# Attention with random features and a two-GEMM expert: products summed in PSUM, and projections in 64 rows

## The chip, the cores and the metric

The kernel runs on one core of one Trainium2 chip. A core has a matrix engine (PE; its weight loads are listed as PEld), a vector engine (DVE), an activation engine (ACT), GpSimd (POOL) and a queue processor (SP) that issues the DMAs here. PE writes its sums into PSUM, which the kernel uses as eight banks of 128 x 512 float32 values; DVE and ACT read them out. The metric is the device time of one execution, in microseconds; lower is better.

## The reference

```python
def _attn_ref(q, k, v, omega):            # q, k, v: (8, 8, 576, 64), omega: (128, 64)
    m, D = omega.shape
    scale = 1.0 / np.sqrt(np.sqrt(D))
    q_s, k_s = (q * scale, k * scale)
    def phi(x):
        proj = np.einsum('bhsd,md->bhsm', x, omega)
        sq = np.sum(x * x, axis=-1, keepdims=True) / 2.0
        h = proj - sq
        h = h - np.max(h, axis=-1, keepdims=True)
        return np.exp(h) / np.sqrt(m)
    q_p, k_p = (phi(q_s), phi(k_s))
    kv = np.einsum('bhsm,bhsd->bhmd', k_p, v)
    z = np.sum(k_p, axis=2)
    num = np.einsum('bhsm,bhmd->bhsd', q_p, kv)
    den = np.einsum('bhsm,bhm->bhs', q_p, z)[..., None] + 1e-06
    return (num / den).astype(np.float32)

def _moe_ref(x, w_in, w_out):             # x: (4608, 512) from the attention, w_in: (512, 2048)
    h = x @ w_in                          # GEMM 1
    sp = np.maximum(h, 0.0) + np.log1p(np.exp(-np.abs(h)))
    g = h * erf(sp)
    return (g @ w_out).astype(np.float32) # GEMM 2
```

## The kernel before

**Attention.** Two heads make a pair: 32 pairs, four per batch, 2 x 576 tokens each, which are nine chunks of 128 tokens. The fifth chunk (MID) holds the end of one head and the start of the other. For q and for k the tile `u` has 64 rows of data and 64 rows of their squares (`square`, mostly on POOL), so that one product of 128 rows with `wq` or `wk` (`project`, three chunks per PSUM bank `pp`) gives the projection less the squares. `maximum` (DVE) takes the largest feature of each token, `exponential` (ACT) writes `f`. Then `key_values` sums `kvp`, `turn` transposes `fq` into `pt`, and `attend` makes `nd` (numerators and denominators) in two halves of 288 columns per head. From pair 8 on (WHOLE) operands are split into a high and a low part, and a product is three matmuls: high by high, high by low, low by high. ACT takes log and exponential of the denominators (`rc`), DVE multiplies.

**The expert.** Every batch goes through GEMM 1 and GEMM 2 in two phases; in the trace their PSUM tiles begin with `h` and `o`. In a phase GEMM 1 has four granules (`f` 0 to 3), each of two 128-row blocks by 576 columns. In batches 0 to 2 (`plain1`, PLAIN) a granule is four sums of two products. From batch 3 on (`gemm1`) it is seven products of sums of blocks (PRODUCTS), each of six matmuls of 288 columns, each in a PSUM bank of its own (`hA...`, `hS...`). Banks of GEMM 1 are limited to three at once (CAPS `moe1`). The products are put together in SBUF: one is copied to `hs`, the others are added by DVE, some to two places, with `u2` in between. `chain` applies softplus, erf, the gate (`gs`, `hs`), and splits into `gh` and `gl` for GEMM 2.

**Weights.** A weight arrives as 64-bit words, which `make` turns into float32: `w_bias` (POOL or ACT), a shift and two bit operations (DVE), then `parts` splits high and low (`w_high`, `w_rest`; ACT or POOL, DVE or POOL). This is done once for each of 32 units, from the start to some 243 us, and each made unit is stored in device memory (`wdw`). Later uses fetch it: a unit is 512 KB, a block half of that. A granule of `gemm1` fetches three units and a block.

**The order.** All operations are handed to a planner (`Plan.order`), with costs (COST, LAG), due times, the engines that may run each, and limits on tiles at once (SLOTS, CAPS). It simulates the engines and writes out one fixed order for each of them; an engine runs its list in that order and waits on semaphores. BLOCKS sets how granules of GEMM 1 and output tiles of GEMM 2 (`e`, of the phase before) follow each other; attention of later batches is placed between by due time.

```python
PRODUCTS = (("A11", "B11", (((0, 0), None),)),
            ("S2", "T2", (("U2", (0, 0)),)),
            ("S3", "T3", (((1, 0), "U2"),)),
BLOCKS = (("f", 0), ("f", 1), ("e", 0), ("f", 2), ("e", 1), ("f", 3), ("e", 2), ("e", 3))
```

Every instruction goes through one helper, so nearly all rows of the profile name line 742; tiles tell them apart.

Of the kernel before, what the change touches and what calls it, by code (L numbers as in the profile page):

```python
# [25 lines left out]
D1 = D + 1  # L26
DM, DF = 512, 2048
# [22 lines left out]
PRODUCTS = (("A11", "B11", (((0, 0), None),)),  # L50
            ("S2", "T2", (("U2", (0, 0)),)),
            ("S3", "T3", (((1, 0), "U2"),)),
            ("A12", "B21", (((0, 0), (0, 0)),)),
            ("S1", "T1", (((1, 1), (1, 0)), ((0, 1), "U2"))),
            ("A22", "T4", (((1, 0), (1, 0)),)),
            ("S4", "B22", (((0, 1), (0, 1)),)))


COST = dict(mm=0.132, proj=0.222, tr=0.109, kv=0.222, table=1.3)
LAG = {"T": 0.35, "A": 0.25, "V": 0.25, "G": 0.3, "S": 0.3}  # L60
SLOTS = dict(w=8, u=3, f=2, mx=3, v=2, qh=1, ql=1, kh=1, kl=1, rc=2, xs=4, xh=2, xl=2, u2=2,
             hs=4, gs=2, gh=6, gl=6, os=4, ps=8)
CAPS = dict(st=2, wt=2, cv=2, att=4, moe1=3, moe2=2)
# [26 lines left out]
class Plan:  # L90
# [43 lines left out]
    def order(self, slots, caps):  # L134
# [187 lines left out]
def build(emit):  # L322
# [36 lines left out]
    def parts(t, src, keys):  # L359

        ks = range(2)
        pl.op("whigh", [("A", 0.63, -1e9), ("G", 0.7, WHG)], lambda e: E.w_high(e, t, src),
              reads=keys, writes=[(t, ("h", k)) for k in ks])
        pl.op("wrest", [("V", 0.68, -1e9), ("G", 1.3, 3.0)], lambda e: E.w_rest(e, t, src),
              reads=keys + [(t, ("h", k)) for k in ks], writes=[(t, ("l", k)) for k in ks])

    def make(u, t):
# [8 lines left out]
        pl.op("wshift", [("V", 0.42, -1e9)], lambda e: E.w_shift(w), reads=[(w, 0)], writes=[(w, 0)])  # L376
        pl.op("wsign", [("V", 0.69, -1e9)], lambda e: E.w_sign(st, w), reads=[(st, 0), (w, 0)],
              writes=[(w, 0)])
        pl.op("wtail", [("V", 0.69, -1e9)], lambda e: E.w_tail(st, w), reads=[(st, 0), (w, 0)],
              writes=[(w, 0)])  # L380
        parts(t, lambda: w.ap.bitcast(F32).rearrange("p (k c) -> p k c", k=2), [(w, 0)])
        store(u, t)

    def unit(u, block=None):

        count[0] += 1
        t = pl.tile("w", "w%s_%d" % ("_".join(str(c) for c in u), count[0]),
                    [P, 2 if block is None else 1, 2, BW], F32R,
                    cap=SLOTS["w"] - CAPS["cv"] if clock[0] < starts[2 * PLAIN + 1] else None)
        if u not in stored:  # L390
            make(u, t)
        else:
            d = stored[u]
            fetch(u, t, lambda: d.ap if block is None else d.ap[:, block:block + 1])
# [25 lines left out]
    def weights1(b, ph, fp):  # L420
        if b < PLAIN:
            t0, t1 = (unit(("1", ph, 2 * fp + i)) for i in range(2))
            if b == PLAIN - 1:
                make_sums(ph, fp, t0, t1)
            return {"A11": (t0, 0), "A12": (t0, 1), "A21": (t1, 0), "A22": (t1, 1)}
        t0, s0, s1 = unit(("1", ph, 2 * fp)), unit(("S", ph, fp, 0)), unit(("S", ph, fp, 1))
        t1 = unit(("1", ph, 2 * fp + 1), 1)
        return {"A11": (t0, 0), "A12": (t0, 1), "A22": (t1, 0), "S2": (s0, 0), "S3": (s0, 1),
                "S1": (s1, 0), "S4": (s1, 1)}
# [8 lines left out]
    def early(n):  # L438
        return 5 if n < NP else None

    def load(n, qk):
        a = pairs[n]

        u = a["u" + qk] = pl.tile("hs", f"u{qk}{a['nm']}", [P, S2], F32, "u0") if 0 < n < NP else \
            pl.tile("u", f"u{qk}{a['nm']}", [P, S2])
        parts = 3 if n == 0 else 1
        for i in range(parts):
# [3 lines left out]
        if qk == "k":  # L451
            v = a["v"] = pl.tile("v", "v" + a["nm"], [P, (NC + 1) * D1])
            pl.op("loadv", [("S", 0.1, 1e9)], lambda e: E.v_load(v, a), writes=[(v, 0)],
                  size=P * (NC + 1) * D1 * 4)
        for i in range(parts):
# [7 lines left out]
    def project(n, qk, t0):  # L463
# [5 lines left out]
        for i in range(3):  # L469
            pp = pl.tile("ps", f"pp{qk}{a['nm']}_{i}", [P, 512], F32, "att", early(n))  # L470
            pl.op("proj" + qk, [("T", 3 * COST["proj"], -1e9)], lambda e, i=i, pp=pp: E.project(pp, u, qk, i),
                  reads=[(u, ("x", i)), (u, ("s", i))], writes=[(pp, 0)],
                  plan=pair_time(n, t0 + 0.05 * i))
            pl.op("max" + qk, [("V", 0.56, -1e9)], lambda e, i=i, pp=pp: E.maximum(mx, pp, i),
                  reads=[(pp, 0)], writes=[(mx, i)])
            pl.op("exp" + qk, [("A", 1.1, -1e9)], lambda e, i=i, pp=pp: E.exponential(f, mx, pp, i),
                  reads=[(pp, 0), (mx, i)], writes=[(f, i)], set="exp")

    def key_values(n, t0):
# [16 lines left out]
    def turn(n, t0):  # L496
# [15 lines left out]
    def attend(n, t0):  # L512
        a = pairs[n]
        x = xs[n] = pl.tile("xs", f"xs{a['nm']}", [P, 2, T])
        for j in range(2):
            for t in range(2):
                nd = pl.tile("ps", f"nd{a['nm']}_{j}_{t}", [P, 512], F32, "att", early(n))
                rc = pl.tile("rc", f"rc{a['nm']}_{j}_{t}", [P, T])
                c = range((j * S + t * T) // 384, (j * S + (t + 1) * T - 1) // 384 + 1)
                pl.op("nd", [("T", 0.5 if n < WHOLE else 3 * COST["mm"], -1e9)],  # L520
                      lambda e, j=j, t=t, nd=nd: E.attend(nd, a["kh"], a["kl"], a["qh"], a["ql"], j, t),
                      reads=[(a["kh"], 0), (a["kl"], 0)] + [(a["qh"], i) for i in c]
                      + [(a["ql"], i) for i in c], writes=[(nd, 0)],
                      plan=pair_time(n, t0 + 0.1 * j + 0.05 * t))
                pl.op("ndlog", [("A", 0.5, -1e9)], lambda e, j=j, nd=nd, rc=rc: E.log_den(rc, nd, j),
                      reads=[(nd, 0)], writes=[(rc, 0)], set="exp")
                pl.op("ndexp", [("A", 0.44, -1e9)], lambda e, j=j, rc=rc: E.exp_den(rc, j),
                      reads=[(rc, 0)], writes=[(rc, 0)], set="exp")
                pl.op("divide", [("V", 0.47, -1e9)], lambda e, j=j, t=t, nd=nd, rc=rc: E.divide(x, nd, rc, j, t),
                      reads=[(nd, 0), (rc, 0)], writes=[(x, (j, t))])  # L530
# [53 lines left out]
    def product(hp, where, wn, b, names, xn, more, end):  # L584

        unit_, k = where[wn]
# [9 lines left out]
    def plain1(b, ph, fp):  # L596
        where = weights1(b, ph, fp)
# [438 lines left out]
```

## Time and profile before

| | |
|---|---|
| median of 3 runs | 1103.88 us (1101.33 to 1104.65) |
| the profiled execution | span 1101.4 us from first to last instruction; its device time is not listed apart |
| PE busy | 1074.1 us, 98% |
| DVE, ACT, POOL busy | 715.1, 709.0, 435.1 us |
| granted PE clock | 0.988 in the mean, 0.93 in the first 140 us |
| data moved by DMA | 231.27 MB, mean 210 GB/s |

The profiled span is 2.5 us below the median of the runs. A row of the timeline has the start, the time to the modelled end, engine, line, operation, out<-in, shape and count; what stands in brackets is the idle time before it and what ended it. A plain float32 matmul shows as two records, one of the split operands (high or low) as one.

### The profile page before, as it was taken

What the parts mean: (1) busy time and instruction counts of PE and PEld (TensorE: products, weight loads), DVE (VectorE), ACT (ScalarE), POOL (GpSimd) and SP (SyncE); (2) the same over time, 40 slices, a digit from 0 to 9 for tenths busy, and PEclk for the clock granted to TensorE, in tenths of its full rate; (3) what the DMA queues carried; (4) which work ended last, traced back from release to release, by engine and by line L of the source; (5) the groups of instructions that cost most, each with busy time, mean ns of one, the idle gap of its engine ahead of it and who ended that gap; (6) DMA issues with size and microseconds to landing.
All of it is one profiled execution on the core that took longest, in us unless ns stands there. A gap on an engine that the chain in (4) does not pass through costs nothing.

```text
span 1101.4 us, 21514 instructions
## 1 busy us (share of the span) xinstructions
PE 1074.1 (98%) x8272; PEld 1063.9 (97%) x8272; DVE 715.1 (65%) x1257; ACT 709.0 (64%) x1354; POOL 435.1 (40%) x353
## 2 busy tenths in 40 slices
PE   7798899999999999999999999999999999999998
PEld 6698899999999999999999999999999999999998
DVE  5967789876377575955757566675656766464541
ACT  7777769776578766756647667476566764654440
POOL 6535336210075294822436343343334413252300
PEclk9899899999999999999999999999999999999999
DMA  8546568675557666666666777657765666567771
GB/s 241 174 132 205 173 231 279 198 257 162 171 176 251 205 204 242 190 215 226 216 211 207 225 216 222 211 181 247 232 225 185 214 216 208 193 226 278 254 241 58
DMA packets 70117, 231.27 MB, mean 210 GB/s; under 512 B 8288, under 2 KB 8672, under 8 KB 70016
## 3 DMA queue, kind: packets, MB, share of 16 engines
q1 hardware_dynamic: 69952, 229.84, 63.9%
q8 instruction: 66, 1.08, 0.4%
q14 instruction: 35, 0.29, 0.1%
q0 software_dynamic: 64, 0.07, 0.0%
HBM read 195.26 MB, written 34.60 MB: 209 GB/s over the span
## 4 chain that ended last, share of the span: by engine, by line
PE 91%; DVE 4%; ACT 1%; issue 1%; DMA 1%; SPq 1%; POOL 0%; DVEq 0%
PE o L742 36%; PE h L742 13%; PE hS L742 11%; PE hA L742 8%; PE ppq L742 5%; PE kvp L742 5%; PE ppk L742 5%; PE nd L742 5%; PE pt L742 2%; DVE wt L742 1%; DMA uk<-kT 1%; SPq L742 1%; DVE qh L742 0%; DVE hs L742 0%; DVE mxk L742 0%
## 5 line engine op out<-in xcount | busy, mean ns | idle before, releaser
L742 PE MATMUL o<-gh,w 128*128 128x288 f32 x2048 | 444.8, 298 | 7.8 <-POOL w L742 7.4
L742 PEld LDWEIGHTS o<-gh,w 128*128 128x128 f32 x2048 | 338.9, 188 | 9.0 <-POOL w L742 8.0
L742 PE MATMUL o<-gl,w 128*128 128x288 f32 x1024 | 301.9, 295 | 0.0
L742 PEld LDWEIGHTS o<-gl,w 128*128 128x128 f32 x1024 | 192.7, 188 | 0.2
L742 PE MATMUL h<-xh,w 128*128 128x288 f32 x768 | 178.8, 305 | 0.9 <-ACT hs L742 0.9
L742 PE MATMUL hS<-xh,wS 128*128 128x288 f32 x640 | 165.7, 302 | 1.1 <-issue 1.1
L742 ACT ACTIVATE fk<-ppk,mxk 128x128 f32<-128x128 f32 x288 | 83.3, 371 | 78.0 <-DVE mxk L742 77.6
L742 PEld LDWEIGHTS h<-xh,w 128*128 128x128 f32 x768 | 131.2, 191 | 1.6 <-ACT hs L742 1.3
L742 PE MATMUL hA<-xh,w 128*128 128x288 f32 x480 | 122.1, 299 | 0.0
L742 ACT ACT_TABLE_LOAD x92 | 118.0, 1283 | 2.4 <-PEq L1027 0.7
L742 PEld LDWEIGHTS hS<-xh,wS 128*128 128x128 f32 x640 | 114.8, 189 | 1.3 <-issue 1.3
L742 PE MATMUL h<-xl,w 128*128 128x288 f32 x384 | 113.9, 297 | 0.0
L742 ACT ACTIVATE fq<-ppq,mxq 128x128 f32<-128x128 f32 x288 | 83.2, 371 | 40.0 <-DVE mxq L742 39.5
L742 POOL TENSOR_TENSOR gl<-hs,gh 128x576 fp32r<-128x576 f32 x50 | 86.5, 1753 | 42.2 <-ACT gh L742 25.8
L742 POOL TENSOR_TENSOR uq<-uq 64x576 f32<-64x576 f32 x40 | 46.4, 1178 | 139.6 <-DMA uq<-qT 98.1
L742 POOL TENSOR_TENSOR hs<-gs,hs 128x576 f32<-128x576 f32 x40 | 65.1, 1649 | 85.8 <-ACT gs L742 66.0
L742 DVE TENSOR_REDUCE mxk<-ppk 128x3 f32<-128x384 f32 x96 | 52.8, 556 | 68.9 <-PE ppk L742 67.8
L742 PE MATMUL hS<-xl,wS 128*128 128x288 f32 x320 | 94.5, 295 | 0.0
L742 POOL TENSOR_TENSOR uk<-uk 64x576 f32<-64x576 f32 x44 | 53.5, 1234 | 93.1 <-DMA uk<-kT 91.6
L742 ACT ACTIVATE gh<-hs 128x1152 fp32r<-128x1152 f32 x49 | 56.4, 1164 | 48.1 <-DVE hs L742 19.4
L742 PEld LDWEIGHTS hA<-xh,w 128*128 128x128 f32 x480 | 85.9, 189 | 0.0
L742 PE MATMUL ppk<-wk,uk 128*128 128x128 f32 x576 | 79.2, 279 | 4.4 <-DVE wk L742 4.1
(94 smaller groups left out, 2124.4 us busy)
## 6 DMA issues: line engine op xcount, KB each, us to landing
w<-wdw SPq DMA_DIRECT2D x184, 512.0 KB, 4.3
wS<-wdcS SPq DMA_DIRECT2D x80, 512.0 KB, 4.0
st<-w SPq DMA_DIRECT2D x32, 512.0 KB, 5.2
wdw<-w SPq DMA_DIRECT2D x32, 512.0 KB, 3.9
v<-vP SPq DMA_DIRECT2D x32, 325.0 KB, 3.5
w<-wdw SPq DMA_DIRECT2D x40, 256.0 KB, 3.7
out<-os SPq DMA_DIRECT2D x32, 288.0 KB, 4.0
uk<-kT SPq DMA_DIRECT2D x31, 288.0 KB, 4.2
```

The source lines that it names most:

```text
L742: return tc.keep_in_program_order(method(*args, **kwargs))
```

## The change

- Projections of pairs 8 to 31 (ROWS): the data of both heads lie beneath each other in 64 rows each, without squares. For the four chunks of each head that hold one head alone, `project_rows` issues eight matmuls of 64 rows, by turns for the upper and the lower rows and into two banks; the MID chunk has both heads in 128 rows with zeros (`project_mid`). The squares go another way: q and k are loaded a second time with tokens on partitions (`tokens_load`), squared (POOL), summed by a DVE reduction, and subtracted from the maxima (`shift`).
- Attention's columns are cut into 384 and 192 in place of 288 and 288, and the exponential of the denominators covers both heads in one instruction.
- GEMM 1 from batch 3 on: the seven products go into three banks X, Y and Z and are summed there by PE; X gets four of them and is read out after each, Y two. Four read-outs are copies (ACT or DVE), three are additions (DVE).
- Its weights come in blocks of 256 KB (512 KB tiles of two, fetched apart), in order of use (UNITS).
- Granules 0 and 1 of a phase are issued by turns (`merged`). Up to five banks may be GEMM 1's.
- `make` keeps its tile in PSUM (CAPS `wp`, two banks), and its operations are no longer offered to POOL: bias and the high part go to ACT, the rest to DVE. Attention of the first four pairs may hold seven banks, before five.

```diff
-PRODUCTS = (("A11", "B11", (((0, 0), None),)),
...
+PRODUCTS = (("X", "A11", "B11", (0, 0), 0),
+            ("Y", "S1", "T1", (1, 1), 0),
+            ("X", "S2", "T2", (0, 1), 0),
+            ("Z", "A12", "B21", (0, 0), 1),
+            ("X", "S3", "T3", (1, 1), 1),
+            ("Y", "S4", "B22", (0, 1), 1),
+            ("X", "A22", "T4", (1, 0), 0))
+UNITS = (("A11", "S1"), ("S2", "S4"), ("S3", "A12"), ("A22",))
-CAPS = dict(st=2, wt=2, cv=2, att=4, moe1=3, moe2=2)
+CAPS = dict(st=2, wt=2, wp=2, cv=2, att=4, moe1=5, moe2=2)
+SPANS = ((0, 384), (384, 192))
+BLOCKS = ((("f", 0), ("f", 1)), (("e", 0),), (("f", 2),), (("e", 1),), (("f", 3),), (("e", 2),), (("e", 3),))
+ROWS = 8
...
     def make(u, t):
-        w = pl.tile("gh", f"wt{nm}", [P, HW], I32, "wt")
-        pl.op("wbias", [("G", 0.8, WBG), ("A", 0.67, -1e9)], lambda e: E.w_bias(e, st, w),
+        w = pl.tile("ps", f"wt{nm}", [P, HW], I32, "wp")
+        pl.op("pbias", [("A", 0.67, -1e9)], lambda e: E.w_bias(e, st, w),
...
     def early(n):
-        return 5 if n < NP else None
+        return 7 if n < NP else None
...
     def load(n, qk):
+        if rows:
+            pl.op("load" + qk, [("S", 0.1, 1e9)], lambda e: E.rows_load(u, qk, a), writes=[(u, "x")],
+                  size=P * (WIDE + P) * 4)
+            pl.op("load" + qk, [("S", 0.1, 1e9)], lambda e: E.tokens_load(u, qk, a), writes=[(u, "t")],
+                  size=P * NC * D * 4)
...
     def gemm1(b, ph, fp):
+            first = bank not in banks
+            if first:
+                banks[bank] = pl.tile("ps", f"h{bank}{b}_{ph}_{fp}", [P, 512], F32, "moe1")
+            hp = banks[bank]
+            product(hp, where[wn], b, XB, xn, 0 if first else 2, 1)
+            if plus:
+                pl.op("hadd", [("V", 0.46, -1e9)], lambda e: E.h_add(hs.ap[:, to[0], to[1], :], hp),
+                      reads=[(hp, 0), (hs, to)], writes=[(hs, to)])
+            else:
+                pl.op("hout", [("A", 0.42, -1e9), ("V", 0.46, 0.0)],
...
+        def project_rows(self, low, high, u, qk):
+            x = u.ap[:, NC * D:]
+            for c in range(MID):
+                for r, b in ((slice(0, D), low), (slice(D, P), high)):
+                    pe.matmul(b.ap[:, c * P:(c + 1) * P], lhsT=x[r, c * P:(c + 1) * P], rhs=wr[r],
+                              start=True, stop=True)
+
+        def project_mid(self, b, u, qk):
+            pe.matmul(b.ap[:, :P], lhsT=u.ap[:, NC * D + WIDE:], rhs=wr, start=True, stop=True)
+        def shift(self, mx, sq):
+
+            for x in (-half_sq, half_sq):
+                dve.scalar_tensor_tensor(mx.ap, sq.ap, x, mx.ap, op0=ALU.mult, op1=ALU.add)
```

PE's order at the q projection of pair 3 of batch 4 (tile `ppq_4_3`), before: three groups of three chunks, with GEMM 1 products between them.

```order
L742 MATMUL ppq_4_3_0_6445<-wq_70,uq_4_3_5987 128x128 x3
...
L742 MATMUL hS33_1_1_6476<-xh3_0_5324,wS_1_1_0_118_6228 128x288
L742 MATMUL ppq_4_3_1_6485<-wq_70,uq_4_3_5987 128x128 x3
L742 MATMUL hS33_1_1_6476<-xh3_1_5334,wS_1_1_0_118_6228 128x288
...
L742 MATMUL hS13_1_1_6507<-xh3_0_5324,wS_1_1_1_119_6267 128x288
L742 MATMUL ppq_4_3_2_6514<-wq_70,uq_4_3_5987 128x128 x3
L742 MATMUL hS13_1_1_6507<-xh3_1_5334,wS_1_1_1_119_6267 128x288
...
L742 MATMUL kvp_4_3_6529<-v_4_3_5782,fk_4_3_6360 128x2x65
```

The same projection in the changed kernel (`ppq_4_3_0` and `_2` are the banks of the upper and the lower rows, `_1` that of the MID chunk, `wr` the scaled omega on both halves of the rows):

```order
L824 MATMUL o3_0_0_0_6559<-gh3_0_1_6326,w2_0_0_0_121_6402 128x288
...
L824 MATMUL ppq_4_3_0_6577<-wr_72,uq_4_3_6015 128x128
L824 MATMUL ppq_4_3_2_6578<-wr_72,uq_4_3_6015 128x128
...
L824 MATMUL ppq_4_3_1_6593<-wr_72,uq_4_3_6015 128x128
L824 MATMUL kvp_4_3_6595<-v_4_3_5828,fk_4_3_6456 128x2x65
L824 MATMUL kvp_4_3_6595<-v_4_3_5828,fk_4_3_6456 128x65 x4
```

The eight matmuls of 64 rows now follow each other without anything between and form one block per projection.

PE's order in granule 2 of batch 4, phase 0, before: each product has its own bank, named after its weight block (the first row of each).

```order
L742 MATMUL hA114_0_2_7453<-xh4_0_6955,w1_0_4_147_7194 128x288
...
L742 MATMUL hS24_0_2_7463<-xh4_0_6955,wS_0_2_0_148_7230 128x288
...
L742 MATMUL hS34_0_2_7473<-xh4_0_6955,wS_0_2_0_148_7230 128x288
...
L742 MATMUL hA124_0_2_7482<-xh4_0_6955,w1_0_4_147_7194 128x288
```

The same granule changed, with the first row of each product and what lies before X's third and fourth:

```order
L824 MATMUL hX4_0_2_7455<-xh4_0_6970,wb147_7292 128x288
...
L824 MATMUL hY4_0_2_7469<-xh4_0_6970,wb147_7292 128x288
...
L824 MATMUL hZ4_0_2_7483<-xh4_0_6970,wb149_7335 128x288
...
L824 MATMUL hX4_0_2_7455<-xh4_0_6970,wb148_7310 128x288
...
L824 MATMUL hY4_0_2_7469<-xh4_0_6970,wb148_7310 128x288
...
L824 MATMUL ppq_5_1_1_7523<-wr_72,uq_5_1_6832 128x128
L824 MATMUL hX4_0_2_7455<-xh4_0_6970,wb149_7335 128x288
```

Between two products into X the planner puts products into Y and Z, or matmuls of GEMM 2 and of attention; the same X bank comes back four times.

POOL's order while the first weights are made, before (`wt` is the tile being made, `w` the finished unit):

```order
L742 TENSOR_SCALAR wt1_0_2_342<-st1_0_2_279 128x512
L742 TENSOR_TENSOR uq_0_3_302<-uq_0_3_302 64x576 x2
L742 TENSOR_SCALAR w1_0_1_2_158<-wt1_0_1_269 128x2x256
L742 TENSOR_TENSOR w1_0_1_2_158<-wt1_0_1_269,w1_0_1_2_158 128x2x256
L742 TENSOR_SCALAR wt1_0_3_417<-st1_0_3_384 128x512
```

And changed:

```order
L824 TENSOR_TENSOR uk_0_3_225<-uk_0_3_225 64x576 x2
L824 TENSOR_TENSOR uq_0_3_280<-uq_0_3_280 64x576 x2
L824 TENSOR_SCALAR xh0_0_581<-xs_0_2_526 128x576
L824 TENSOR_SCALAR xh0_0_581<-xs_0_0_325 128x576
L824 TENSOR_TENSOR xl0_0_601<-xs_0_2_526,xh0_0_581 128x288 x2
```

The rows of `wt` and `w` have left POOL for ACT and DVE.

More of the change, by code (lines that the diff above doesn't have):

```diff
@@ L393, in unit, with blocks @@
             d = stored[u]
-            fetch(u, t, lambda: d.ap if block is None else d.ap[:, block:block + 1])
+            fetch(u, t, lambda: d.ap, (0, 1), 2)
+        return t
+    def blocks(us):
+        cap = room()
+        t = pl.tile("w", "wb%d" % count[0], [P, len(us), 2, BW], F32R, cap=cap)
+        for k, (u, i) in enumerate(us):
+            d = stored[u]
+            fetch(u, t, lambda d=d, i=i: d.ap[:, i:i + 1], (k,), 1)
         return t
@@ L468, in project @@
         mx = pl.tile("mx", f"mx{qk}{a['nm']}", [P, NC])
[L469 to L477, printed above, removed]
+        rows = n >= ROWS
@@ new lines, in project @@
+        for i in order:
+            c = chunks[i]
+            pl.op("max" + qk, [("V", 0.15 + 0.135 * len(c), -1e9)],
+                  lambda e, i=i, c=c: E.maximum(mx, banks[i], c),
+                  reads=[(banks[i], 0)], writes=[(mx, k) for k in c])
+        if rows:
+            sq = a["s" + qk]
+            pl.op("less", [("V", 0.33, -1e9)], lambda e: E.shift(mx, sq),
+                  reads=[(mx, k) for k in range(NC)] + [(sq, 0)], writes=[(mx, k) for k in range(NC)])
+        for i in order:
+            c = chunks[i]
+            pl.op("exp" + qk, [("A", 0.371 * len(c), -1e9)],
+                  lambda e, i=i, c=c: E.exponential(f, mx, banks[i], c),
+                  reads=[(banks[i], 0)] + [(mx, k) for k in c], writes=[(f, k) for k in c], set="exp")
@@ L582, in build, with product @@
     group = {x: {0: 0, 1: 0, 2: 2, 3: 2 if x is XPLAIN else 3, 4: 3, 5: 3, 6: 3} for x in (XB, XPLAIN)}
-    def product(hp, where, wn, b, names, xn, more, end):
-        unit_, k = where[wn]
+    def product(hp, w, b, names, xn, more, end):
+        unit_, k = w
         xi = names.index(xn)
@@ new lines, in one @@
+        def one(bank, wn, xn, to, plus):
+            if wn not in where:
+                us = next(x for x in UNITS if wn in x)
+                t = blocks([source(ph, fp, x) for x in us])
+                where.update({x: (t, i) for i, x in enumerate(us)})
+            first = bank not in banks
[6 more added lines that the diff above has]
+                      reads=[(hp, 0), (hs, to)], writes=[(hs, to)])
+            else:
+                pl.op("hout", [("A", 0.42, -1e9), ("V", 0.46, 0.0)],
+                      lambda e: E.h_out(e, hs.ap[:, to[0], to[1], :], hp), reads=[(hp, 0)],
+                      writes=[(hs, to)])
@@ L633, in build @@
+        return [lambda x=x: one(*x) for x in PRODUCTS]
     macros = [0]
@@ L689, in build @@
+        return [lambda h=h, t=t, fi=fi: one(h, t, fi) for h in range(2) for t in range(2)
+                for fi in range(FT // 2)]
     clock = [START0, 1.0]
@@ L694, in at, with merged @@
         return now
+    def merged(lists):
+        steps = sorted((((i + 0.5) / len(x), j, i) for j, x in enumerate(lists) for i in range(len(x))))
+        for _, j, i in steps:
+            lists[j][i]()
     for n in range(NP):
@@ L719, in build, with tile_attention_moe @@
     for e in range(KT):
[L720 removed]
+        merged([gemm2(*last, e)])
     return pl
 @with_exitstack
[L725 removed]
+def tile_attention_moe(ctx: ExitStack, tc: tile.TileContext, qT, kT, qR, kR, qN, kN, vP, omT, w1, w2, out):
     nc = tc.nc
```

303 lines of the change are left out of this document (174 added, 129 removed).

## The prediction

> **What bounds the kernel now.** First I read the page's head and its chain of work that ended last, then busy time by stretches (start:end, length, then PE, weight loads, DVE, ACT and POOL busy, granted clock, DMA share, GB/s), then PE's waits.
>
> ```profile
> span 1101.4 us, 21514 instructions
> PE 1074.1 (98%) x8272; PEld 1063.9 (97%) x8272; DVE 715.1 (65%) x1257; ACT 709.0 (64%) x1354; POOL 435.1 (40%) x353
> PE 91%; DVE 4%; ACT 1%; issue 1%; DMA 1%; SPq 1%; POOL 0%; DVEq 0%
> 0.00:140.00 140.00, 119.43 (x848) 111.80 (x849) 105.08 (x168) 107.72 (x244) 70.41 (x73) 0.93 0.59 186
> 48.00:243.00 195.00, 183.73 (x1383) 179.39 (x1382) 156.34 (x236) 149.77 (x305) 79.08 (x77) 0.96 0.62 206
> 820.00:890.00 70.00, 70.00 (x554) 70.00 (x552) 46.01 (x88) 44.15 (x85) 28.42 (x22) 1.00 0.66 212
> PE o L742 <- POOL w L742: 7.4, 2, 6.9
> PE nd L742 <- DVE qh L742: 6.8, 6, 2.5
> ```
>
> PE carries 91% of the chain. From 820 to 890 us it is busy throughout, DVE for 46 us of 70 and ACT for 44: there only less PE work saves time. PE's idle time lies mostly in the first 140 us (20.6 us), where the granted clock is also low, 0.93. So PE's work is counted first, then that first stretch.
>
> **The 64-row projections.** PE's cadence is taken from starts, because ends are modelled (the row of 288 is from the chain, the last from the tile ppq, the others from the timeline).
>
> ```profile
> 96.36 2.17 PE L742 MATMUL ppk<-wk,uk 128*128 128x128 f32 x18
> 98.37 0.49 PE L742 MATMUL pt<-ident,fq 128*128 128x128 f32 x3
> 577.70 1.23 PE L742 MATMUL kvp<-v,fk 128*128 128x130 f32 x10
> 578.74 0.38 PE L742 MATMUL hS<-xh,wS 128*128 128x288 f32 x1
> 578.95 0.29 PE L742 MATMUL hS<-xl,wS 128*128 128x288 f32 x1
> 1059.42 38.13 PE o L742 x288
> L742 PE MATMUL ppq<-wq,uq x576: 270/275/377, 7.7 to 934.4; 128*128 128x128 f32 x192
> ```
>
> Eighteen projection records go by in 98.37 - 96.36 = 2.01 us, 0.112 us each; a chunk has two records, so nine chunks take 2.01 us. A 288-column record takes 38.13 / 288 = 0.132 us. The ten kvp records (65 or 130 columns) take 578.95 - 577.70 - 0.132 = 1.12 us, again 0.112 each: at these widths a record lasts as long as its weight load, whatever its columns. A 128-column pass itself is 0.132 x 128 / 288 = 0.059 us (estimate).
>
> There are 24 pairs x 2 = 48 projections. In each, eight of the nine chunks (128 rows of stationary data, 64 of them squares; 16 records, 1.79 us) become eight matmuls of 64 rows, again 16 records, which go by turns to the upper and the lower rows of the array; the ninth chunk stays at 128 rows and 0.22 us. No row here shows a 64-row matmul, so it is bounded:
> - best: two halves run wholly side by side, 0.112 us per two records, 0.89 us; saved 0.89 x 48 = 42.9 us.
> - worst: nothing overlaps, 1.79 us as now, and entering and leaving the divided array each lets the pipe run empty, for which the nearest row is a record's length over its cadence, 0.275 - 0.112 = 0.163 us: lost 2 x 0.163 x 48 = 15.7 us.
> - taken: within its own rows a half must load (0.112) and then pass (0.059), while the other rows do the same beside it: (0.112 + 0.059) / 2 = 0.085 per record, 16 x 0.085 = 1.36 us, saved 0.42 x 48 = **20.3 us**. The drain I leave at nothing: the change of kind that a row does show, kvp to hS, costs none (that is the sum above, with 0.112 per record to the last).
>
> The Trainium skill, "TensorEngine Tiling (Array Packing)", Key Properties, says that changing the tiling mode drains the engine, whereas going from tile to tile doesn't. No run here shows it yet; by that rule, at the drain priced above, 15.7 of the 20.3 us would be lost again (the second rival).
>
> ```profile
> L742 DVE TENSOR_REDUCE mxq<-ppq x96: 541/558/561, 8.5 to 934.7; 128x3 f32<-128x384 f32 x96
> ```
>
> DVE gets a sum of squares per projection, 0.558 x 576 / 384 = 0.84 us (estimate), and two corrections of nine columns; the maxima keep their total width. POOL's square now holds up these corrections and no longer the projection. All nine exponentials wait for three maxima and the sum, so three of the four attention banks are held longer, and behind them kvp and pt on PE. All this costs nothing as long as GEMM products stand in PE's queue meanwhile and DVE has room, as the 820 us row shows (46 of 70); without that cover a projection would expose the 0.84 us, 40 us in all.
>
> **Attention's 384 and 192 columns.** Of 24 x 12 = 288 nd records at 0.132, half become 384 wide (0.132 x 384 / 288 = 0.176) and half 192 wide (0.088 by width, 0.112 by the load). 144 x (0.176 + 0.112 - 0.264) = **+3.5 us**; by width alone 0. I take the load, since kvp shows it.
>
> **The weights' making.** POOL's share of the 32 units moves to ACT and DVE.
>
> ```profile
> 113.12 0.61 PE L742 MATMUL o<-gh,w 128*128 128x288 f32 x1 [6.88 <-POOL w L742]
> L742 DVE SCALAR_TENSOR_TENSOR wt<-st,wt x64: 674/693/1801, 20.5 to 240.8; 128x512 int32<-128x512 int32 x64
> L742 DVE TENSOR_SCALAR wt<-wt x32: 410/422/1478, 20.0 to 239.7; 128x512 int32<-128x512 int32 x32
> L742 POOL TENSOR_SCALAR wt<-st x27: 641/665/1757, 19.3 to 237.0; 128x512 f32<-128x512 f32 x27
> L742 POOL TENSOR_SCALAR w<-wt x20: 617/618/1663, 31.8 to 241.7; 128x512 fp32r<-128x512 f32 x20
> L742 POOL TENSOR_TENSOR w<-wt,w x18: 1254/1292/1653, 32.5 to 234.3; 128x512 fp32r<-128x512 f32 x18
> L742 DVE TENSOR_TENSOR w<-wt,w x14: 674/683/1281, 23.4 to 242.3; 128x512 fp32r<-128x512 f32 x14
> L742 ACT ACTIVATE w<-wt x12: 613/631/633, 22.3 to 236.3; 128x512 fp32r<-128x512 f32 x12
> L742 ACT ACTIVATE wt<-st x5: 662/682/695, 75.0 to 221.0; 128x512 f32<-128x512 f32 x5
> L742 ACT ACTIVATE rc<-nd,eps 64x288 f32<-64x288 f32 x128 | 58.8, 492 | 27.2 <-PE nd L742 18.4 <-DVE xs L742 7.5
> L742 ACT ACTIVATE rc<-rc 64x288 f32<-64x288 f32 x128 | 51.7, 436 | 2.2
> ```
>
> GEMM 2's first weights came late off POOL (6.88 us), and POOL no longer touches them: **-7 us**. If this fails, ACT or DVE is late instead. Load from 48 to 243 us: ACT gains 27 x 0.68 + 20 x 0.63 = 31 us and gives back two of a pair's four 0.436 us exponentials of rc (the two left cover the same columns on twice the partitions), 0.87 us on some 12 pairs, 10 us: 150 + 21 = 171 of 195. DVE gains 18 x 0.68 = 12 and 32 x (0.69 - 0.42) = 9 for the shift at PSUM (estimate from its neighbours), and may lose the 1.8 us outliers that fall beside POOL: 156 + up to 21 = 177. Both fit; I count 0, with ends of 7 us gained (the 6.8 us on qh, since the first pairs may hold more banks) and 18 lost (a rival below).
>
> **GEMM 1's banks.** The matmuls stay; per granule eight evacuations and adds become seven, and of all of them DVE's rows fall from 332 to 208 while ACT's rise from 84 to 166. New is that X's next product waits until X's last one is read out.
>
> ```profile
> 546.31 0.29 PE L742 MATMUL hA<-xh,w 128*128 128x288 f32 x1
> 546.65 0.46 DVE L742 TENSOR_TENSOR hs<-hA,hs 128x288 f32<-128x288 f32 x1 [1.01 <-PE hA L742]
> L742 ACT ACTIVATE gs<-hs x64: 1144/1164/1174, 85.1 to 1059.9; 128x1152 f32<-128x1152 f32 x64
> PE h L742 <- ACT hs L742: 0.9, 1, 0.9
> PE o L742 <- DMA w<-wdw: 0.2, 1, 0.2
> ```
>
> From a product's last matmul (546.31) to the end of its read-out (547.11) is 0.80 us, of which 0.67 lie behind its own 0.132. In the order the shortest of 160 re-entries have nine matmuls in between, 1.19 us: 35 of them. The three banks taken in turn before had 31 re-uses at just that distance, and of all of PE's waits on a read-out there is one, 0.9 us. So 0; that 0.9 is the most that could be gained, and the other end is a rival.
>
> **DMA.** Each projection loads 327 KB of rows beside 295 KB of tokens: 15.7 MB more, and weights come in 256 KB blocks.
>
> ```profile
> GB/s 241 174 132 205 173 231 279 198 257 162 171 176 251 205 204 242 190 215 226 216 211 207 225 216 222 211 181 247 232 225 185 214 216 208 193 226 278 254 241 58
> DMA packets 70117, 231.27 MB, mean 210 GB/s; under 512 B 8288, under 2 KB 8672, under 8 KB 70016
> w<-wdw SPq DMA_DIRECT2D x184, 512.0 KB, 4.3
> w<-wdw SPq DMA_DIRECT2D x40, 256.0 KB, 3.7
> ```
>
> 247 MB in 1080 us are 229 GB/s, below the 278 and 279 of single slices, and a block of 256 KB lands in 3.7 us where a whole unit took 4.3. SP issues 168 rows more (682 for 514), in an order that runs ahead of use: cost 0. If that cover fails, each of 40 granules waits for a landing of at most 3.7 us; PE's list of waits now has 0.2 us on DMA.
>
> **Sum.** 1101.4 - 20.3 - 7 + 3.5 = 1077.6 us of span. The median of the runs, 1103.9, lies 2.5 above this profiled execution: 1080.
>
> **Rivals.**
> - Full overlap: -42.9 in place of -20.3, 1058 us. For it: the load sets the pace in kvp, and halves in different rows load different cells. Against: no row shows two loads at once. The Trainium skill, "TensorE: Matmul & The Clock Gate", Part 3, lets loads and matmuls of different row groups overlap, at a few ns per further tile; by that rule this is the outcome, and no run here shows it yet.
> - Half overlap with a drain at each entry and exit: 15.7 us more than forecast, 1096 us.
> - Serial halves with drains: +15.7 in place of -20.3, 1116 us, **slower**. For it: the loads here follow each other at 0.112 us and never two at once. It decides from 1.94 us for the eight halves, where 0.15 x 48 = 7 us of loss eat the -7 + 3.5 and 3.3 more. Serial without drains: 1101 us.
> - ACT and DVE late in batches 0 and 1: if the idle share of the first 140 us (15%) held from 48 to 243 us, where it is 6% now, 18 us come back, 1098 us. For it: POOL falls idle where ACT would be at 88% and DVE at up to 91%. Against: PE ran at 94% there with both near 80%.
> - Bank waits: if the 71 re-entries below 1.6 us each found the reading engine at the start of a 1.16 us activation, they would wait 0.67 + 1.16 - 1.19 = 0.64 us, 45 us in all; a third of that gives 1095 us. Against: the 31 re-uses before.
>
> **Chances.** Forecast 0.42 (1070 to 1090 by itself); full overlap 0.18; half overlap with drains 0.12; ACT and DVE late 0.07; bank waits 0.05; serial without drains 0.07, with drains 0.09. What a measurement here can tell from no change is 0.3%, 3.3 us. Faster: 0.42 + 0.18 + 0.12 + 0.06 + 0.04 = 0.82; same 0.08; slower 0.10. The range takes in full overlap up to 5 us past its middle and the drains and late cases up to 1100; the serial halves stay outside: 1053 to 1100.
>
> **What will show it.** Cadence of the 64-row ppq and ppk records: 0.085 right, 0.056 full overlap, 0.112 serial; a gap over 0.1 us around them means drains. The 6.9 us wait on POOL's w gone, and no DVE or ACT wait of its size up to 250 us. PE still without idle time from 820 us on; waits of hX on ACT or DVE would show the banks. The forecast is wrong above all if the halves don't overlap.

## The result and the profile after

The changed kernel takes 1076.72 us (median of 4 runs, 1073.78 to 1078.61) and the kernel before, measured beside it, 1103.57 us (1101.33 to 1104.65): a ratio of 0.9756 [0.9740, 0.9772], 27 us faster. The profiled execution has a span of 1072.0 us, so 29.4 us lie between the two spans shown. It is the fastest of the four; a second profile of the same kernel, taken later, has a span of 1075.0 us. Where that matters, both are given.

The head of the page, and by engine the chain of work that ended last:

```profile
span 1072.0 us, 21687 instructions
PE 1051.2 (98%) x8272; PEld 1025.9 (96%) x8272; DVE 734.6 (69%) x1316; ACT 719.4 (67%) x1390; POOL 352.1 (33%) x306
PE 92%; DMA 3%; DVE 3%; ACT 1%; issue 1%; SPq 0%; POOL 0%; DVEq 0%; POOLq 0%; ACTq 0%
```

Busy time by the same three stretches as before (columns as there):

```profile
0.00:140.00 140.00, 124.76 (x892) 115.17 (x893) 114.12 (x205) 116.57 (x265) 41.46 (x45) 0.99 0.63 200
48.00:243.00 195.00, 186.75 (x1423) 178.23 (x1423) 169.45 (x290) 157.66 (x313) 38.62 (x42) 0.99 0.69 236
820.00:890.00 70.00, 70.00 (x563) 68.85 (x562) 47.17 (x88) 48.02 (x93) 22.86 (x16) 1.00 0.65 222
```

PE's waits (us in total, times, longest):

```profile
PE ppk L824 <- DVE wk L824: 4.2, 1, 4.2
PE h L824 <- DVE w L824: 2.8, 3, 1.6
PE nd L824 <- DVE qh L824: 1.8, 4, 0.7
PE h L824 <- ACT w L824: 1.6, 1, 1.6
...
PE h L824 <- DMA w<-wdw: 0.5, 1, 0.5
```

PE still carries the chain (92%) and still has no idle time from 820 to 890 us. The 7 us row on POOL's `w` is gone and the one on DVE's `qh` is down from 6.8 to 1.8 us; in the first 140 us PE's idle time fell from 20.6 to 15.2 us and the granted clock rose from 0.93 to 0.99. Between 48 and 243 us DVE is at 169 of 195 us and ACT at 158, where the prediction had 177 at most and 171.

The 64-row records by form (busy time, mean ns of one | idle before):

```profile
L824 PE MATMUL ppk<-wr,uk 64*128 64x128 f32 x384 | 27.9, 285 | 0.0
L824 PE MATMUL ppq<-wr,uq 64*128 64x128 f32 x384 | 27.9, 285 | 0.0
```

One block of them in PE's timeline, with its neighbours:

```profile
576.45 0.29 PE L824 MATMUL o<-gh,w 128*128 128x288 f32 x1
576.67 1.16 PE L824 MATMUL ppk<-wr,uk 64*128 64x128 f32 x16
577.76 0.40 PE L824 MATMUL hY<-xh,wb 128*128 128x288 f32 x1
578.00 0.30 PE L824 MATMUL hY<-xl,wb 128*128 128x288 f32 x1
```

The block: 576.45 to 578.00 is 1.55 us; less the 0.132 us that the record before it and the one behind it take anyway, 1.29 us for 16 records, where the kernel before took 16 x 0.112 = 1.79. So 0.50 x 48 = 24 us. The starts inside this block, in us from its first record:

```
before   -0.222 (o)
pairs     0.000 0.007 | 0.213 0.220 | 0.325 0.332 | 0.437 0.443
          0.548 0.555 | 0.660 0.667 | 0.772 0.778 | 0.883 0.890
behind    1.092 (hY)  1.332 (hY)
```

An upper and a lower record start 7 ns apart, and from pair to pair it is 0.112 us, the time of one load: full overlap, 0.056 per record. But the block is entered late (0.222 in place of 0.132 us, and 0.213 in place of 0.112 from the first pair to the second) and left late (0.202 from the last record in place of 0.112, and 0.240 in place of 0.132 behind it): 0.09 + 0.10 + 0.09 + 0.11 = 0.39 us for the two changes together. All 48 blocks have the same 0.890 us from the first start to the last.

Attention's columns and the making of the weights, by tile (durations least, median, longest, in ns):

```profile
L824 PE MATMUL nd<-qh,kh x160: 247/332/591, 16.3 to 927.5; 128*128 128x384 f32 x80, 128*128 128x192 f32 x80
L824 DVE SCALAR_TENSOR_TENSOR wt<-st,wt x64: 681/695/730, 21.6 to 237.4; 128x512 int32<-128x512 int32 x64
L824 ACT ACTIVATE wt<-st x32: 608/636/692, 19.3 to 233.8; 128x512 f32<-128x512 f32 x32
L824 DVE TENSOR_SCALAR wt<-wt x32: 686/693/700, 20.0 to 234.5; 128x512 int32<-128x512 int32 x32
```

The shift on PSUM takes 0.69 us, as estimated (0.42 before), and the outliers of 1.8 us beside POOL have gone from these rows (longest 0.73).

Where the 29.4 us went, by PE's records (each from its start to the next one's, at most 0.6 us of it; what exceeds 0.6 is idle time), us:

| | before | after |
|---|---|---|
| projections of 128 rows | 122.4 | 48.4 |
| projections of 64 rows | - | 52.4 |
| kvp, pt, nd | 60.0, 31.4, 58.1 | 61.2, 27.5, 59.4 |
| GEMM 1, GEMM 2 | 390.8, 415.2 | 391.3, 416.1 |
| idle | 15.3 | 7.3 |

Projections -21.6 (the record ahead of a block, which is delayed too, may stand in another row), idle time -8.0. In the second profile the idle time is 9.9 us, so -5.4: some 3 us of this row differ from one execution to the next. A lower granted clock makes records longer, so its part stands in their rows.

### The profile page after: what moved, and what is told of

It reads as the page before. It is cut to its first block, busy times and chain, and to the rows that moved or that the text cites. A ratio compares the mean times of both kernels' runs of the same rounds, so it can differ in the third digit from the quotient of the medians.

```text
span 1072.0 us, 21687 instructions
## 1 busy us (share of the span) xinstructions
PE 1051.2 (98%) x8272; PEld 1025.9 (96%) x8272; DVE 734.6 (69%) x1316; ACT 719.4 (67%) x1390; POOL 352.1 (33%) x306
## 4 chain that ended last, share of the span: by engine, by line
PE 92%; DMA 3%; DVE 3%; ACT 1%; issue 1%; SPq 0%; POOL 0%; DVEq 0%; POOLq 0%; ACTq 0%
PE o L824 37%; PE h L824 13%; PE hX L824 12%; PE hY L824 6%; PE kvp L824 5%; PE nd L824 5%; PE ppq L824 4%; PE ppk L824 4%; PE hZ L824 3%; PE pt L824 2%; DMA st<-w 1%; DVE wt L824 1%; DMA uq<-qN 1%; DMA w<-wdw 1%; DVE xs L824 0%
## 5 line engine op out<-in xcount | busy, mean ns | idle before, releaser
L824 PE MATMUL hX<-xh,wb 128*128 128x288 f32 x640 | 162.0, 299 | 0.0
L824 PEld LDWEIGHTS hX<-xh,wb 128*128 128x128 f32 x640 | 113.5, 188 | 0.4
L824 POOL TENSOR_TENSOR uk<-uk 128x288 f32<-128x288 f32 (+1 forms) x54 | 49.4, 934 | 181.4 <-DMA uk<-kN 119.9
L824 POOL TENSOR_TENSOR uq<-uq 128x288 f32<-128x288 f32 (+1 forms) x46 | 42.4, 942 | 184.5 <-DMA uq<-qN 66.1
L824 POOL TENSOR_TENSOR gl<-hs,gh 128x576 fp32r<-128x576 f32 x50 | 89.4, 1809 | 39.7 <-ACT gh L824 29.4
L824 PE MATMUL hX<-xl,wb 128*128 128x288 f32 x320 | 94.6, 296 | 0.0
L824 DVE TENSOR_REDUCE mxk<-ppk 128x4 f32<-128x512 f32 (+2 forms) x96 | 50.7, 553 | 62.1 <-PE ppk L824 61.1
L824 POOL TENSOR_TENSOR hs<-gs,hs 128x576 f32<-128x576 f32 x26 | 42.9, 1669 | 149.5 <-ACT gs L824 149.5
L824 DVE TENSOR_TENSOR hs<-gs,hs 128x1152 f32<-128x1152 f32 x51 | 81.2, 1600 | 13.4 <-ACT gs L824 13.4
L824 ACT ACTIVATE hs<-hX 128x288 f32<-128x288 f32 x75 | 30.8, 410 | 85.8 <-PE hX L824 82.9
L824 ACT ACTIVATE rc<-nd,eps 64x192 f32<-64x192 f32 (+1 forms) x128 | 63.6, 497 | 33.3 <-PE nd L824 30.7
L824 PE MATMUL hY<-xh,wb 128*128 128x288 f32 x320 | 81.3, 299 | 0.0
```

Source lines behind the costliest of these rows:

```text
L824: return tc.keep_in_program_order(method(*args, **kwargs))
```

## The experiments

The time differences below are differences of ratios to the kernel before, times 1103 us; the intervals make them uncertain by some 2 to 3 us. "The changed kernel" is the mean of its two measurements where nothing else is said.

**All projections in 128 rows.** Does the gain come from the projections at all?

```diff
-ROWS = 8
+ROWS = 32
```

> The changed kernel with every projection as before the change (128 rows, squares in the stationary data, three thirds in three banks); all else stays changed. Theory A (halves fully side by side, but each entry into and exit from the divided array costs, together 0.39 us): a projection's eight chunks take 1.79 us again in place of 1.29, 0.50 x 48 = 24 us more than the changed kernel's 1076.7, 1101 us. Theory B (as predicted: 0.085 us per record, no such cost): 20 us more, 1097 us. Rival C (most of the gain lies in the first 250 us, in the weights' making and the banks): under 10 us more, below 1087 us.

1101.76 us, ratio 0.9990 [0.9978, 1.0002]: not told apart from the kernel before. PE's projections take 126.2 us again. Without the 64 rows the rest of the change brings nothing that can be measured; with them the kernel is 25 to 26 us faster.

**Four upper, then four lower matmuls.** Is it the turns that overlap the halves?

```diff
-            for c in range(MID):
-                for r, b in ((slice(0, D), low), (slice(D, P), high)):
+            for r, b in ((slice(0, D), low), (slice(D, P), high)):
+                for c in range(MID):
```

> The changed kernel, but project_rows issues the four matmuls of the upper rows first and then the four of the lower rows, instead of by turns. Theory A: two halves run side by side only when they follow each other; without turns each record again takes its weight load, 0.112 us, 16 x 0.112 = 1.79 in place of 0.89: 0.9 x 48 = 43 us more, 1120 us, with records of 64 rows 0.11 us apart. Rival D (the queue finds the other rows' matmuls by itself, the order within the block doesn't matter): 1077 us, pairs 0.007 us apart.

1101.73 us, ratio 0.9992 [0.9980, 1.0004]: the gain is lost, but neither number was met. The 64-row records by form:

```profile
L824 PE MATMUL ppk<-wr,uk 64*128 64x128 f32 x384 | 41.0, 285 | 0.0
```

A block in PE's timeline:

```profile
590.75 0.29 PE L824 MATMUL o<-gh,w 128*128 128x288 f32 x1
590.98 1.71 PE L824 MATMUL ppk<-wr,uk 64*128 64x128 f32 x16
592.62 0.40 PE L824 MATMUL hY<-xh,wb 128*128 128x288 f32 x1
592.86 0.29 PE L824 MATMUL hY<-xl,wb 128*128 128x288 f32 x1
```

The block takes 592.86 - 590.75 (the record before) - 0.264 = 1.85 us. Its starts:

```
 0.000 0.213 0.326 0.437 0.548 0.554 | 0.660 0.768 0.773 | 0.879 0.884 0.992
 1.103 1.215 1.326 1.438 | behind 1.640
```

Upper records alone go by at 0.112; around the change of halves three pairs still start 5 or 6 ns apart, because lower records are begun beside upper ones that stand ahead of them: the record with the first of the block's two completion signals, the last of the upper half, is the eleventh to start, at 0.884, so three of the lower half have started before it. So 16 records with three overlaps, 13 x 0.112 = 1.46, and the same 0.39 for entry and exit: 1.85. That is the sum of both effects.

**Two blocks of eight records.** The MID chunk's 128-row matmul is put between the fourth and the fifth 64-row matmul, so that the array's division is entered and left twice per projection.

```diff
-            pl.op("proj" + qk, [("T", 8 * COST["half"], -1e9)],
-                  lambda e: E.project_rows(banks[0], banks[2], u, qk),
...
+            pl.op("proj" + qk, [("T", 8 * COST["half"] + COST["proj"], -1e9)],
+                  lambda e: (E.project_rows(banks[0], banks[2], u, qk, 0), E.project_mid(banks[1], u, qk),
+                             E.project_rows(banks[0], banks[2], u, qk, 1)),
...
-            for c in range(MID):
+            for c in range(2 * i, 2 * i + 2):
```

> The changed kernel, but the MID chunk (128 rows) is issued between the fourth and the fifth of the eight halves, so that the array is divided and made whole again twice per projection. The matmuls are the same. Theory A: one more entry and exit, 0.39 us x 48 = 19 us more, 1095 us (some less, since the MID chunk stood directly behind the halves in 19 of 48 projections already). Theory B (no cost of changing): 1077 us.

1093.43 us, ratio 0.9910 [0.9891, 0.9929]: 17 us slower for 48 more entries and exits, 0.36 us each. Entry and exit are a price of their own, and the time gives nearly the 0.39 us read from the starts. It lies where the edit is: PE's projection records (64 and 128 rows) take 119.9 us, in the two profiles of the changed kernel 100.8 and 102.0.

**The changed kernel again**, nothing changed, as a base on the chip of the next three.

> The changed kernel itself once more, as the yardstick for the three beside it: 1077 us, within 0.3%.

1075.67 us, ratio 0.9751 [0.9736, 0.9766].

**Products in banks of their own.** GEMM 1's seven products go into separate banks as in the kernel before, and DVE adds them; everything else of the change stays.

```diff
-PRODUCTS = (("X", "A11", "B11", (0, 0), 0),
-            ("Y", "S1", "T1", (1, 1), 0),
...
+PRODUCTS = (("A11", "B11", (((0, 0), None),)),
+            ("S2", "T2", (("U2", (0, 0)),)),
...
-UNITS = (("A11", "S1"), ("S2", "S4"), ("S3", "A12"), ("A22",))
+UNITS = (("A11", "A12"), ("S2", "S3"), ("S1", "S4"), ("A22",))
...
+            hp = pl.tile("ps", f"h{wn}{b}_{ph}_{fp}", [P, 512], F32, "moe1")
+            product(hp, where[wn], b, XB, xn, 0, 1)
+            for to, plus in outs:
```

> The changed kernel with GEMM 1's seven products again in a bank each, put together by DVE as before the change (the sum that went through u2 is kept in the granule's own tile); blocks fetched apart, granules by turns and the five banks stay. If the summing in banks neither saves nor costs PE time, as predicted: 1077 us, with DVE busier by some 50 us in all. If re-entries into X's bank cost PE time: faster than 1074 us. If the summing gave part of the gain by relieving DVE: above 1080 us with DVE waits in PE's list.

1095.73 us, ratio 0.9933 [0.9912, 0.9953]: 20 us slower. DVE is busy for 775 us in place of 735. PE's longest wait in the list of waits:

```profile
PE hA L830 <- DVE hs L830: 9.9, 5, 2.8
```

One such stall in the timelines of DVE, POOL and PE:

```profile
585.26 2.75 DVE L830 SCALAR_TENSOR_TENSOR mxk<-sk,mxk 128x9 f32<-128x9 f32 x2
587.93 0.44 DVE L830 TENSOR_TENSOR hs<-hS,hs 128x288 f32<-128x288 f32 x1
585.23 2.75 POOL L830 TENSOR_TENSOR gl<-hs,gh 128x576 fp32r<-128x576 f32 x2 [1.88 <-ACT gh L830]
588.43 0.61 PE L830 MATMUL hA<-xh,wb 128*128 128x288 f32 x1 [2.79 <-DVE hs L830]
```

The stretches around it (the last three columns: granted clock, DMA share, GB/s):

```profile
584.80:588.40 3.60, 0.55 (x3) 0.31 (x3) 3.53 (x6) 1.99 (x4) 3.17 (x3) 0.87 0.91 297
588.40:592.00 3.60, 3.57 (x15) 3.56 (x16) 3.14 (x8) 2.08 (x9) 0.83 (x2) 0.50 0.55 214
592.00:596.00 4.00, 4.00 (x24) 4.00 (x23) 2.27 (x6) 1.41 (x3) 0.00 (x0) 0.72 0.57 205
```

A bank has to be added by DVE before PE may use it again. DVE's queue has the correction of the maxima ahead, nine columns, and that lasts as long as POOL's two operations beside it, 2.75 us. PE stands for 2.79 us, and then goes on at a granted clock of 0.50 and 0.72 for some 7 us.

Such a stall comes three times, at 585, 718 and 852 us, and the granted clock has a mean of 0.72, 0.70 and 0.72 over some 12 us from each on. About 2.8 us of waiting and 12 x 0.28 = 3.4 us of lost clock, three times, are 18.6 of the 20 us (estimate).

**The weights made in SBUF with POOL's help**, as before.

```diff
-        w = pl.tile("ps", f"wt{nm}", [P, HW], I32, "wp")
-        pl.op("pbias", [("A", 0.67, -1e9)], lambda e: E.w_bias(e, st, w),
+        w = pl.tile("gh", f"wt{nm}", [P, HW], I32, "wt")
+        pl.op("wbias", [("G", 0.8, WBG), ("A", 0.67, -1e9)], lambda e: E.w_bias(e, st, w),
```

> The changed kernel with the weights made in SBUF as before the change, POOL sharing bias, high part and rest. If POOL's lateness cost the 7 us that the prediction took back: 1084 us, with a wait on POOL's w of some 7 us about 100 to 120 us. If the new order (granules 0 and 1 by turns, so that GEMM 2's first product comes later) already hides it: 1077 us, or faster by the 2 to 4 us that PE now waits on DVE's and ACT's w.

1082.98 us, ratio 0.9816 [0.9800, 0.9831]: 7 us slower, in size what the prediction had. But the wait isn't on POOL's `w`:

```profile
PE h L822 <- ACT hs L822: 7.3, 1, 7.3
```

It stands at 108 us and is a read-out of GEMM 1 queued on ACT; a later one, of 2.6 us on ACT's `gs`, stands at 173 us. Which engine is late there depends on the planner's order; that one is late is what the two kernels share.

**Columns 288 and 288.**

```diff
-SPANS = ((0, 384), (384, 192))
+SPANS = ((0, 288), (288, 288))
```

> The changed kernel with attention's columns cut into 288 and 288 again in place of 384 and 192; the exponential still covers both heads. If 192-column matmuls last as long as their weight load (0.11 us), as predicted: 144 x (0.174 + 0.111 - 0.264) = 3 us less PE work, 1073.7 us. If their time goes by width: 1077 us.

1074.78 us, ratio 0.9746 [0.9730, 0.9762]: by the ratios 0.6 us less than the changed kernel beside it, which isn't told apart. PE's nd records take 55.7 us for 59.4, so the 3.7 us are there, but idle time over 0.6 us is 11.4 for 9.9. It is the lowest median of all versions, within the measurement of the changed kernel.

**Granules 0 and 1 one after the other.** The runs with own banks left a question: do they cost by themselves, or only since the two granules are issued by turns?

```diff
-BLOCKS = ((("f", 0), ("f", 1)), (("e", 0),), ...
+BLOCKS = ((("f", 0),), (("f", 1),), (("e", 0),), ...
```

> The changed kernel, with GEMM 1's granules 0 and 1 of a batch one after the other instead of product by product by turns. Theory T (the turns give every re-entry of a bank its distance): without them a product begins sooner after the same bank's last read-out, PE waits on the read-out (a row of PE on hs well above the 1 us in all of the changed kernel), and the time rises by some 5 to 15 us over 1076, to 1081-1091. Rival N (nine matmuls, 1.19 us, are enough against a 0.8 us read-out, whatever stands around): 1076, within 2 us, no new row of waits. Both predict the 64-row blocks unchanged at 1.29 us.

1083.92 us, ratio 0.9833 [0.9814, 0.9853]: 8.7 us slower. The time is in theory T's range, its mechanism in part:

```profile
PE h L824 <- DVE w L824: 6.7, 3, 4.2
...
PE h L824 <- DVE hs L824: 2.6, 2, 1.8
...
PE hY L824 <- DVE hs L824: 1.2, 1, 1.2
PE hX L824 <- ACT hs L824: 1.0, 3, 0.5
```

2.2 us are waits of X and Y on their read-outs. Another 2.6 us, on read-outs by DVE in the first 250 us, belong to the plain GEMM 1; the changed kernel has no such row. PE's wait for DVE's `w` grew by 3.9 us. Other waits became shorter; in all, PE's idle time over 0.6 us is 15.4 us, where the two profiles of the changed kernel have 7.3 and 9.9, so 5.5 to 8 of the 8.7 us are waits. What brings those outside X and Y isn't shown.

**Own banks, and granules one after the other**: both edits.

> The kernel with the seven products in banks of their own, added by DVE (1095.7 us), with granules 0 and 1 of a batch one after the other, as in the kernel before. Theory B (the added read-outs and sums by themselves make DVE and ACT late, and the 2.75 us stall beside POOL's sums is part of it): still 1090 or more, and the stalls of some 3 us once per batch remain. Rival M (the two granules by turns are what crowds the read-outs, own banks alone cost nothing, as in the kernel before): 1076-1080 and no stall of that size.

1096.40 us, ratio 0.9943 [0.9923, 0.9964]: as slow as with turns, and 12 us slower than the summed banks without turns. So B: the read-outs and sums cost with and without the turns. The place of the stall moves: in the timelines of PE and DVE, `pt` now waits for DVE's `ql`, which stands behind a correction and a subtraction of GEMM 2's input:

```profile
462.76 0.44 PE L830 MATMUL pt<-ident,fq 128*128 128x128 f32 x2 [3.00 <-DVE ql L830]
459.40 1.57 DVE L830 SCALAR_TENSOR_TENSOR mxk<-sk,mxk 128x9 f32<-128x9 f32 x2
460.89 1.35 DVE L830 TENSOR_TENSOR gl<-hs,gh 128x1152 fp32r<-128x1152 f32 x1
462.16 0.54 DVE L830 TENSOR_TENSOR ql<-pt,qh 128x384 fp32r<-128x384 f32 x1
```

**Own banks, and all projections in 128 rows.** If own banks cost 20 us, why did the kernel with summed banks and 128 rows gain nothing?

```diff
-ROWS = 8
+ROWS = 32
```

> The kernel with the seven products in banks of their own (1095.7 us with 64-row projections, 20 over the changed kernel), with all projections in 128 rows again as in the run of 1101.8 us. Theory P (the added read-outs and sums cost only where PE's own work is short enough to be waited for; 25 us more of projections cover them): 1101-1105, so that the cost shrinks from 20 us to 3 or less, which would say why nothing was gained from the banks without the projections. Rival Q (the sums cost their 20 us under either projections, and another part of the change loses as much): 1118-1122.

1105.63 us, ratio 1.0031 [1.0019, 1.0042]: 4.5 us over the summed banks with 128 rows, not 20. P in kind; the price left is 4.5 where it said 3 or less. Q's 1118 is out. Three stalls come here too, at 596, 728 and 860 us, but shorter ones:

```profile
PE pt L830 <- DVE hs L830: 4.2, 3, 1.4
```

After them the granted clock stays at 1.00. So the price fell because each stall is half as long and costs no clock. Whether the longer projections do that, as P has it, isn't shown: with 128 rows DVE also has no sums of squares and no nine-column corrections (busy for 730 us in place of 775), and no run separates the two.

**The weights made in SBUF, and all projections in 128 rows.**

> The kernel that makes the weights in SBUF with POOL (1083.0 us with 64-row projections, 7.3 over the changed kernel), with all projections in 128 rows again. Theory P (the cover of the longer projections hides part of it): 1102-1105. Rival Q (the waits lie in the first 140 us, where the first pairs hold the 128-row projections in both kernels, so the price stays): 1107-1111.

1102.66 us, ratio 0.9994 [0.9982, 1.0007]: 0.4 us, not told apart from nothing, in place of 7. The time is P's and Q's 1107 is out, but it did not come about by P's mechanism:

```profile
PE h L822 <- ACT hs L822: 7.3, 1, 7.3
```

The same 7.3 us wait stands here, at 107 us, and in the changed kernel the first block of 64 rows begins only at 149 us; so longer projections hide nothing of it. The 2.6 us wait on ACT's `gs` at 173 us is missing here, and the kernel that this one is compared with, 128 rows with the weights made in PSUM, waits 6.8 us on DVE's and ACT's `w`, the changed kernel 4.4. Why all this comes to nothing in the sum isn't shown.

**The 64 rows without either relief**: own banks, granules one after the other, weights made in SBUF.

> The 64-row projections without the two parts that relieve DVE and POOL: products in banks of their own and granules not by turns (1096.4 us), and the weights made in SBUF with POOL's share besides. PE's own work is as short as in the changed kernel. Theory P (what the projections take from PE comes back as waits on DVE and ACT, the two reliefs are what cashes it; their prices add up, 20 + 7 us): 1100-1105, no gain over the kernel before. Rival Q (the prices overlap or lie in different stretches and one hides the other): 1088-1097.

1097.62 us, ratio 0.9945 [0.9926, 0.9964]. Of the 27 us only 6 are left, and the rest of the change (columns, weight blocks, five banks) is still in this kernel. That is just above Q's range and below P's: the prices of the two reliefs do not add up, 21 us together where 20 and 7 stand singly, but nearly all of the gain is gone. The page's head:

```profile
PE 1060.0 (96%) x8272; PEld 1034.2 (94%) x8272; DVE 758.4 (69%) x1391; ACT 676.7 (62%) x1282; POOL 426.1 (39%) x387
```

PE's waits, two of the longest:

```profile
PE h L828 <- ACT hs L828: 8.0, 1, 8.0
PE pt L828 <- DVE ql L828: 6.2, 5, 4.3
```

PE's 64-row records take 52.4 us here as well, so their saving is made; idle time over 0.6 us is 25.9 us in place of 7.3, and the granted clock is 0.985 in the mean for 0.998.

The two-by-two tables that these runs make, us:

| | products summed in PSUM | in banks of their own |
|---|---|---|
| 64 rows | 1076 | 1095.7 |
| 128 rows | 1101.8 | 1105.6 |

| | weights made in PSUM | in SBUF with POOL |
|---|---|---|
| 64 rows | 1076 | 1083.0 |
| 128 rows | 1101.8 | 1102.7 |

## Why the prediction came out as it did

- **64-row projections, -20.3 us.** They gave -24, and the size is nearly right by luck: two errors of opposite sign. The step that failed is "within its own rows a half must load (0.112) and then pass (0.059)": a pair costs one load and nothing for its passes, 0.056 per record, the best end. The other is "The drain I leave at nothing": kvp to hS is a change of shape, not of rows, and could not stand for it; entry and exit take 0.39 us, where the worst end allowed 2 x 0.163. The truth, -42.9 with some 19 back, is the first rival's overlap joined to the second's drain, and no rival joined them. The runs agree with both rules of the Trainium skill that the prediction named: "TensorE: Matmul & The Clock Gate", Part 3 (a few ns from tile to tile; 7 ns here), and "TensorEngine Tiling (Array Packing)", Key Properties (a change of mode drains; 0.39 us for the two here, of which the runs show the time and not what fills it). Taken together, with the drain as the prediction priced it, they would have given 42.9 - 15.7 = 27.2 us, no further off than the 20.3, and for the right reason.
- **Attention's columns, +3.5 us.** The 384-column records stand 0.174 us apart and the 192-column ones 0.111 (forecast 0.176 and 0.112), 144 x (0.174 + 0.111 - 0.264) = +3.0. PE's records give 3.7 us back with 288 and 288; the median hardly moves.
- **The weights' making, -7 us.** The wait on POOL is gone, idle time fell by 8.0 (5.4 in the second profile), and undoing the step costs 7. But with 128-row projections undoing it costs 0.4, though the wait of 7.3 us that comes with it stands in both kernels. So the length of a wait is not, as the sum had it, what its end is worth: by 140 us PE had issued 892 records (867 in the second profile) for 848 before, 5.8 (2.5) us at 0.132. Why the step is worth 7 us only beside the 64 rows stays open.
- **ACT and DVE with POOL's load, 0.** Right: ACT and DVE ran below the forecast loads, and PE's busy share in that stretch rose to 96%.
- **Banks, 0, with "the most that could be gained" 0.9 us.** Read as a step from the kernel before that is nearly right (4.5 us with 128 rows); as a part of this change it is wrong, 12 to 20 us. The step looked for waits on the re-entry of a bank, in a trace where PE was never short of other work. The 124 rows that DVE was rid of were counted in it and then given no value. With the projections 25 us shorter and nine-column corrections in DVE's queue, that room decides; which of the two weighs more isn't shown.
- **DVE's new reductions, "nothing as long as DVE has room".** Right, and the condition named is the one that the runs without the summed banks broke.
- **DMA, 0.** Right: 247 MB at 230 GB/s, and PE's one wait on a weight's transfer, in the plain GEMM 1, is 0.5 us. Waits on the 256 KB blocks do not appear.
- **The sum.** 1077.6 us of span against 1072.0 (1075.0 in the second profile): -3.7 from the projections, -1 from idle time (+1.6), the rest smaller. It held because the change carries its own reliefs. The working added terms that are not additive: with the 64 rows the kernel gains 6 us without the two reliefs and 27 us with them, and without the 64 rows all the rest of the change isn't told apart from nothing. Two slips in the working change nothing: serial halves without drains come to 1100.4 us by its own terms, not 1101, and ACT's rows of read-outs rose to 168, not 166.

## What to carry over

When PE is shortened, ask what its long queue may have been hiding and what the change adds to the other engines, and count the relief of an engine that isn't the bound as a possible condition of the gain, not as a term beside it. A saving on the bound is tested with and without each relief, two by two; undoing one part at a time gives each part the whole interaction. Then look whether the waits changed as the times did: here one price fell with its stalls, the other while its wait stood. Where two mechanisms stand as rivals, ask whether both can hold at once.

## What the runs showed of the chip

- Two matmuls of 64 rows in different halves start 7 ns apart, and a pair costs one load (0.112 us). Going from 128 rows to 64 and back costs 0.36 to 0.39 us, of the 0.90 that full overlap saves on 16 records. So a block of 16 saves 0.50 us, and one of eight 0.06 to 0.09 (4 x 0.112 + 0.36 to 0.39, for 8 x 0.112 = 0.90).
- The overlap does not need strict turns: with all upper records first, three lower ones still started ahead of the last upper one. How far ahead this goes was seen at this one order alone.
- A DVE operation on nine columns can last until a POOL operation on SBUF beside it ends. In the changed kernel, by tile:

```profile
L824 DVE SCALAR_TENSOR_TENSOR mxq<-sq,mxq x48: 170/171/1352, 167.7 to 907.9; 128x9 f32<-128x9 f32 x48
```

  It takes 0.17 us in the median and 1.35 at the longest. Of the 96 such operations (`mxq` and `mxk`) 17 took over 0.4 us, and each of these ended 25 to 31 ns after a POOL operation did; with own banks two of them took the 2.75 us of the two POOL operations. The Trainium skill, "SBUF — State Buffer", section "SBUF: two separate sides", has DVE operations with two SBUF inputs and POOL operations that read SBUF exclude each other for a whole instruction; the rows agree, though no run here took the POOL operation away.
- After PE had stood for 2.79 us, the granted clock was 0.50 for 3.6 us and 0.72 for the next 4: 3.6 x 0.50 + 4 x 0.28 = 2.9 us lost, so the stall cost about twice its length. The two other stalls of that kernel ran alike (0.70 and 0.72 in the mean of some 12 us); after the three waits of at most 1.4 us of the kernel with own banks and 128 rows the clock stayed at 1.00.
